# Products of u and v of two chunks written to four row quarters of PSUM instead of two

## Chip, cores and metric

The kernel runs on one core of a Trainium2 chip. The metric is the device time of one execution in microseconds (us); each version is run several times, and the median is compared.

## What is computed

The reference runs a recurrent attention and then two expert networks over its output. Inputs are r, k, v, w, a, b of shape (4, 8, 768, 40): 4 batches, 8 heads, 768 steps, 40 features, all fp32.

```python
for t in range(S):
    y[:, :, t] = np.einsum('bhd,bhde->bhe', rt, state)
    Sa = np.einsum('bhde,bhe->bhd', state, at)
    state = state * wt[:, :, None, :] - np.einsum('bhd,bhe->bhde', Sa, bt)
    state = state + np.einsum('bhd,bhe->bhde', vt, kt)
x = y.transpose(0, 2, 1, 3).reshape(B * S, H * D)
h = max(x @ w1, x @ w2, x @ w3);  x = h @ w_out          # 320 -> 768 -> 320
h = x @ w_in;  x = (h * tanh(softplus(h))) @ w_out       # 320 -> 2048 -> 320
```

## The kernel before

The recurrence is computed in chunks of 32 steps. The 32 pairs of batch and head are handled as two groups of 16, so there are 2 x 24 = 48 chunks, one after the other (`run`, with `chain(c)` for chunk c); the state goes from each chunk to the next. Inside a chunk everything is matmuls on TensorE (PE), with short steps on VectorE (DVE) and ScalarE (ACT) between them. `chain` has five steps, separated by `yield`:

1. x0ps (line 379): the state times the scaled a of each step, 16 matmuls that write to the four row quarters of a PSUM tile in turn; ACT copies the result to X0 (line 382).
2. ups (line 393): X0 times the inverse of a triangular matrix gives u; DVE copies it to ud (line 395).
3. utps (line 404): u transposed; ACT copies it to uT (line 407, two copies) and into the operand rs (line 410, four copies).
4. `products(c, c + 1)` (line 346): for each of the 16 heads the product of r of chunk c with u of chunk c, and the product of r of chunk c + 1 with v of chunk c + 1. Each is a matmul of 40 rows to 32 columns, with 32 columns moving, fp32. All go to the one PSUM tile cgps (one bank of 128 rows x 512 columns). Then DVE multiplies the 64 rows of chunk c by the causal mask and writes them into rs (line 415, "the mask").
5. ys (line 427): 16 matmuls of the keys and the state with rs; their results are the chunk's output (YT, line 434) and the next state (sv, line 432).

The rows of cgps before: chunk c has the 64 rows from 64 x (c mod 2), the products of v in the first 32 of them and of u in the other 32; a head has 32 of the 512 columns. So one call writes to two of the four row quarters, the u of chunk c to one and the v of chunk c + 1 to one in the other half.

Between these steps other work is put by hand, in a fixed order, in the places where the chain would wait ("slots", five per chunk): the preparation of later chunks (`pre`: lines 239 to 283, with m on PE at line 271), the solve of the triangular systems on DVE (`solve`: lines 303 and 305, eight chunks' worth at a time), `kb` (transposed keys, line 320, copied by ACT at line 324), the copies of the state (line 374), the conversion of the expert weights (lines 564 to 596, craw and raw are their loads), and the first expert network (`Moe1`): groups of eight matmuls into a ring of two PSUM buffers bps (lines 645 to 649), read by ACT (line 752) and DVE (line 754), and later the matmuls of line 795. PE, DVE and ACT keep the order of the code; the order on GpSimd (POOL) and on the DMA queue of SyncE (SP) is set by a scheduler. After the last chunk (some 722 us) the rest of the first network and the second one follow.

Of the kernel before, what the change touches and what calls it, by code (L numbers as in the profile page):

```python
# [12 lines left out]
ALU = mybir.AluOpType  # L13
# [4 lines left out]
C = 32  # L18
# [135 lines left out]
class Attention:  # L154
# [184 lines left out]

    def products(self, h, g):  # L340

        for ho in range(16):
            for c, x, row in ((h, self.uT, 32), (g, self.v, 0)):
                if c is not None:
                    row += 64 * (c % 2)
                    self.nc.tensor.matmul(out=self.cg[row:row + 32, C * ho:C * ho + C], lhsT=x[0:40, ho],  # L346
                                          rhs=self.rs[c % 2][0:40, 0:4, ho], start=True, stop=True)

    ZZ = [(jj, zo, 1 - zo // 2, zo % 2) for jj in range(4) for zo in (0, 2, 1, 3)]

    def chain(self, c):
        nc, tc = self.nc, self.tc
# [3 lines left out]
        x, P = self.ax[n % self.NX], self.pp[n % self.NP][0:R].rearrange("r (p c) t -> r p c t", c=2)[:, :, cc]  # L356
        tt = self.tr[self.batch[n] % 2].rearrange("p t i -> p i t")
        i = c % 2
        l, r_, s, u = self.ls[c % 3], self.rs[i], self.sv[i], self.ud
# [17 lines left out]
        for jj, zo, y, g in self.ZZ:  # L377
            K = 104 if y else (128 if g else 96)
            nc.tensor.matmul(out=ps[32 * zo:32 * zo + 32, 40 * jj:40 * jj + 40], lhsT=x[0:K, y, 4 * g + jj, cc],  # L379
                             rhs=s[0:K, y, 4 * g + jj, 0:40], start=True, stop=True)  # L380
# [10 lines left out]
        for jj, zo, y, g in self.ZZ:  # L391
            zr = slice(32 * zo, 32 * zo + 32)
            nc.tensor.matmul(out=ps[zr, 40 * jj:40 * jj + 40], lhsT=tt[zr, item + jj],
                             rhs=X0[zr, 40 * jj:40 * jj + 40], start=True, stop=True)
# [13 lines left out]
        for zo in range(4):  # L408
# [3 lines left out]
        yield  # L412

        self.products(c, c + 1 if c + 1 < 2 * NCH else None)
        nc.vector.tensor_tensor(  # L415
            out=r_[64:128, 0:4], in0=self.cg[64 * i:64 * i + 64].rearrange("p (h b i) -> p b h i", b=4, i=8),
            in1=self.mask[64:128].rearrange("p (b i) -> p b i", b=4).unsqueeze(2).to_broadcast([64, 4, 16, 8]),
            op=ALU.mult)
        yield
        yield  # L420

# [3 lines left out]
        for p in range(8):  # L425
            for y in (1, 0):
                nc.tensor.matmul(out=self.ys[64 * y:64 * y + 40, p, 0:72], lhsT=l[:, y, p],  # L427
                                 rhs=r_[:, :, 4 * (p % 4) + 2 * (1 - y) + p // 4], start=True, stop=True)
        if not last:
            for y in range(2):  # L430
                ro = slice(64 * y, 64 * y + 40)
                nc.vector.tensor_tensor(out=sn[ro, y, :, 0:40], in0=self.ys[ro, :, 32:72],  # L432
                                        in1=P[ro, :, 32:33].to_broadcast([40, 8, 40]), op=ALU.mult)
# [72 lines left out]
    def run(self, fill):  # L506
# [5 lines left out]
        for c in range(NC):  # L512
            n, cc = divmod(c, 2)
            chain = self.chain(c)
            for slot in range(5):
                if slot == 0 and cc == 0 and self.place[n] == 0 and k == self.batch[n]:
                    finish(solve)
                    left = 0
                next(chain, None)
                if slot == 3 and c + 2 < NC:  # L520
                    self.load_v(c + 2)
# [12 lines left out]
                if left > 0:  # L534
                    steps = -(-left // max(1, 5 * (due - c) - slot - 1))
                    for _ in range(steps):
                        next(solve, None)
                    left -= steps
                next(chain, None)
                if cc == 1 and slot in (0, 2) and n + 1 < NT:  # L540
                    self.kb(n + 1, slot // 2)
# [711 lines left out]
```

## Time and profile before

| | |
|---|---|
| median of 3 runs | 1133.1 us (1131.27 to 1139.1) |
| the profiled execution | 1137.88 us, its span 1136.2 us |
| mean granted clock of TensorE | 0.977 of full speed |
| busy over the span | PE 84%, DVE 78%, ACT 64%, POOL 32% |

Durations come from the one profiled execution. PE's matmuls overlap: a record lasts from its start until its result is there, so the pace of a stream is read from start to start, not from durations. A granted clock of 1.00 is 2.4 GHz, 0.50 is 1.2 GHz.

### The profile page before, as it was taken

What the parts mean: (1) busy time and instruction counts of PE and PEld (TensorE: products, weight loads), DVE (VectorE), ACT (ScalarE), POOL (GpSimd) and SP (SyncE); (2) the same over time, 40 slices, a digit from 0 to 9 for tenths busy, and PEclk for the clock granted to TensorE, in tenths of its full rate; (3) what the DMA queues carried; (4) which work ended last, traced back from release to release, by engine and by line L of the source; (5) the groups of instructions that cost most, each with busy time, mean ns of one, the idle gap of its engine ahead of it and who ended that gap; (6) DMA issues with size and microseconds to landing.
All of it is one profiled execution on the core that took longest, in us unless ns stands there. A gap on an engine that the chain in (4) does not pass through costs nothing.

```text
span 1136.2 us, 33971 instructions
## 1 busy us (share of the span) xinstructions
PE 957.3 (84%) x14098; PEld 859.8 (76%) x14098; DVE 882.6 (78%) x1606; ACT 730.8 (64%) x1886; POOL 366.9 (32%) x394
## 2 busy tenths in 40 slices
PE   1334435898999899988999999988999999999996
PEld 1223324787888888888988888888889998989896
DVE  8778689877768785877576665797898989898885
ACT  3447774454455455545546777666878787878885
POOL 7347785233333334333202334474020102010000
PEclk9999999998999899989998999999999999999999
DMA  8234532333334243423323344441010101010000
GB/s 232 89 87 120 149 77 74 71 97 83 87 90 107 64 106 74 117 66 105 88 66 93 98 128 112 135 142 43 1 52 1 52 1 51 1 52 1 24 1 27
DMA packets 110614, 87.02 MB, mean 77 GB/s; under 512 B 72740, under 2 KB 89764, under 8 KB 110452
## 3 DMA queue, kind: packets, MB, share of 16 engines
q1 hardware_dynamic: 109712, 84.54, 27.3%
q8 instruction: 113, 1.85, 0.7%
q14 instruction: 49, 0.40, 0.1%
q10 hardware_dynamic: 740, 0.23, 0.1%
HBM read 72.16 MB, written 12.58 MB: 75 GB/s over the span
## 4 chain that ended last, share of the span: by engine, by line
PE 57%; DVE 21%; ACT 11%; DMA 4%; issue 4%; POOL 2%; SPq 1%; ACTq 0%; DVEq 0%; POOLq 0%
PE cops L971 5%; PE cops L972 5%; PE cops L973 5%; DVE T L305 4%; PE bps L645 4%; PE cps L645 4%; PE cps L646 4%; PE cps L647 4%; PE cgps L346 3%; PE ys L427 3%; PE bps L795 3%; PE bps L646 3%; PE bps L647 3%; DVE tv L303 3%; ACT ls L324 2%
## 5 line engine op out<-in xcount | busy, mean ns | idle before, releaser
L645 PE MATMUL bps<-bxh,bw 128*128 128x256 f32 x432 | 142.7, 331 | 16.5 <-ACT mx L752 8.6
L646 PE MATMUL bps<-bxl,bw 128*128 128x256 f32 x432 | 126.4, 292 | 4.7 <-DVE bxl L658 4.7
L647 PE MATMUL bps<-bxh,bw 128*128 128x256 f32 x432 | 125.1, 290 | 0.0
L305 DVE TENSOR_TENSOR T<-T,tv 128x31 f32<-128x31 f32 (+15 forms) x186 | 104.4, 561 | 6.4
L645 PEld LDWEIGHTS bps<-bxh,bw 128*128 128x128 f32 x432 | 84.4, 195 | 32.1 <-ACT mx L752 16.6
L757 POOL TENSOR_TENSOR hl<-mx,hh 128x256 fp32r<-128x256 f32 x72 | 57.4, 798 | 156.4 <-ACT hh L756 146.9
L427 PE MATMUL ys<-rs,ls 128*40 128x72 f32 x1536 | 67.2, 249 | 33.2 <-ACT t L572 10.7
L646 PEld LDWEIGHTS bps<-bxl,bw 128*128 128x128 f32 x432 | 85.6, 198 | 7.3 <-DVE bxl L658 7.2
L427 PEld LDWEIGHTS ys<-rs,ls 128*40 128x40 f32 x1536 | 58.7, 131 | 39.8 <-ACT t L572 11.0
L647 PEld LDWEIGHTS bps<-bxh,bw 128*128 128x128 f32 x432 | 85.2, 197 | 0.0
L795 PE MATMUL bps<-hh,bo 128*128 128x256 f32 x360 | 77.4, 297 | 6.8 <-DVE mx L754 5.6
L283 POOL TENSOR_SCALAR_AFFINE_SELECT ax<-akT 32x256 f32<-32x256 f32 x96 | 49.2, 513 | 104.8 <-DVE akT L278 100.8
L382 ACT COPY X<-x0ps 128x160 f32<-128x160 f32 x48 | 14.0, 292 | 104.7 <-PE x0ps L379 98.9
L955 ACT ACTIVATE e<-e 128x512 f32<-128x512 f32 x93 | 58.5, 629 | 35.2 <-DVE e L953 34.7
L959 DVE SCALAR_TENSOR_TENSOR e<-e,r 128x512 f32<-128x512 f32 x93 | 75.1, 808 | 7.6 <-ACT r L957 7.6
L303 DVE TENSOR_TENSOR tv<-tr,T 128x31 f32<-128x31 f32 (+15 forms) x186 | 78.3, 421 | 2.3
L754 DVE TENSOR_TENSOR mx<-bps,mx 128x256 f32<-128x256 f32 x144 | 60.4, 420 | 23.3 <-PE bps L649 13.2
L249 POOL TENSOR_TENSOR ax<-ax,pp 40x512 f32<-40x512 f32 x48 | 62.3, 1298 | 49.0 <-DVE tv L303 15.9
L415 DVE TENSOR_TENSOR rs<-cgps,cst 64x512 f32<-64x512 f32 x48 | 33.1, 689 | 58.0 <-PE cgps L346 57.5
L967 DVE TENSOR_TENSOR gl<-e,gh 128x512 fp32r<-128x512 f32 x93 | 64.6, 695 | 16.3 <-ACT gh L966 15.6
L432 DVE TENSOR_TENSOR sv<-ys,pp 40x320 f32<-40x320 f32 x92 | 44.7, 486 | 38.6 <-PE ys L427 37.9
L924 POOL CAST cxh<-cxl 128x1536 fp32r<-128x1536 f32 x5 | 8.3, 1668 | 197.7 <-DMA cxl<-x 197.7
(210 smaller groups left out, 3296.4 us busy)
## 6 DMA issues: line engine op xcount, KB each, us to landing
bk<-in_KB_dram SPq DMA_DIRECT2D x24, 448.0 KB
sv<-in_SV_dram SPq DMA_DIRECT2D x96, 80.0 KB
raw<-in_w_dram SPq DMA_DIRECT2D x18, 384.0 KB
w<-in_W_dram SPq DMA_DIRECT2D x21, 231.0 KB
v<-in_VT_dram SPq DMA_DIRECT2D x48, 96.0 KB
rs<-in_RT_dram SPq DMA_DIRECT2D x48, 96.0 KB
cxl<-x SPq DMA_DIRECT2D x12, 384.0 KB
raw<-in_wo_dram SPq DMA_DIRECT2D x13, 320.0 KB
```

What stands on the lines that cost most here:

```text
L249: nc.gpsimd.tensor_tensor(out=xv, in0=xv, in1=P[ro, :, 0:C], op=ALU.mult)
L303: nc.vector.tensor_tensor(out=tv, in0=abT[:, s, s + 1:C].unsqueeze(2).to_broadcast([128, n, s + 1]), in1=T[:, s, 0:s + 1].unsqueeze(1).to_ ...
L305: nc.vector.tensor_tensor(out=T[:, s + 1:C, 0:s + 1], in0=T[:, s + 1:C, 0:s + 1], in1=tv, op=ALU.subtract)
L427: nc.tensor.matmul(out=self.ys[64 * y:64 * y + 40, p, 0:72], lhsT=l[:, y, p], rhs=r_[:, :, 4 * (p % 4) + 2 * (1 - y) + p // 4], start=True ...
L645: nc.tensor.matmul(out=ps, lhsT=h[:, k], rhs=xh[:, k], start=(k == 0), stop=False)
L646: nc.tensor.matmul(out=ps, lhsT=h[:, k], rhs=xl[:, k], start=False, stop=False)
L647: nc.tensor.matmul(out=ps, lhsT=l[:, k], rhs=xh[:, k], start=False, stop=False)
L754: after(1, lambda ps=ps, mx=mx: nc.vector.tensor_tensor(out=mx, in0=ps, in1=mx, op=ALU.max))
L795: nc.tensor.matmul(out=pss[d][rows], lhsT=lhsT, rhs=rhs, start=first, stop=last)
L955: nc.scalar.activation(out=e, in_=e, func=AF.Square, bias=1.0)
L959: nc.vector.scalar_tensor_tensor(out=e, in0=e, scalar=1.0, in1=r, op0=ALU.add, op1=ALU.mult)
L967: nc.vector.tensor_tensor(out=gl, in0=e, in1=gh.bitcast(F32), op=ALU.subtract)
```

## The change

Heads 0 to 7 and heads 8 to 15 now have their own rows. A product of the first half goes to rows 0 to 63, one of the second half to rows 64 to 127 (v in the first 32, u in the other 32 of each half); chunk c has the 256 columns from 256 x (c mod 2). The loop takes one head of each half in turn, so that four matmuls in a row write to the four row quarters. The mask becomes two instructions, one for each half of the heads.

```diff
--- before.py
+++ after.py
@@ -339,12 +339,14 @@
 
     def products(self, h, g):
 
-        for ho in range(16):
-            for c, x, row in ((h, self.uT, 32), (g, self.v, 0)):
-                if c is not None:
-                    row += 64 * (c % 2)
-                    self.nc.tensor.matmul(out=self.cg[row:row + 32, C * ho:C * ho + C], lhsT=x[0:40, ho],
-                                          rhs=self.rs[c % 2][0:40, 0:4, ho], start=True, stop=True)
+        for k in range(8):
+            for hi in range(2):
+                for c, x, row in ((h, self.uT, 32), (g, self.v, 0)):
+                    if c is not None:
+                        row += 64 * hi
+                        col = 256 * (c % 2) + C * k
+                        self.nc.tensor.matmul(out=self.cg[row:row + 32, col:col + C], lhsT=x[0:40, 8 * hi + k],
+                                              rhs=self.rs[c % 2][0:40, 0:4, 8 * hi + k], start=True, stop=True)
 
     ZZ = [(jj, zo, 1 - zo // 2, zo % 2) for jj in range(4) for zo in (0, 2, 1, 3)]
 
@@ -412,10 +414,12 @@
         yield
 
         self.products(c, c + 1 if c + 1 < 2 * NCH else None)
-        nc.vector.tensor_tensor(
-            out=r_[64:128, 0:4], in0=self.cg[64 * i:64 * i + 64].rearrange("p (h b i) -> p b h i", b=4, i=8),
-            in1=self.mask[64:128].rearrange("p (b i) -> p b i", b=4).unsqueeze(2).to_broadcast([64, 4, 16, 8]),
-            op=ALU.mult)
+        for hi in range(2):
+            nc.vector.tensor_tensor(
+                out=r_[64:128, 0:4, 8 * hi:8 * hi + 8],
+                in0=self.cg[64 * hi:64 * hi + 64, 256 * i:256 * i + 256].rearrange("p (h b i) -> p b h i", b=4, i=8),
+                in1=self.mask[64:128].rearrange("p (b i) -> p b i", b=4).unsqueeze(2).to_broadcast([64, 4, 8, 8]),
+                op=ALU.mult)
         yield
         yield
 
```

The order on PE of the ys matmuls, the last step of the chunk at 557 us (ys is PSUM, rs_157 the masked operand, ls_153 keys and state; behind "waits" stand the engines or DMA queues waited for). Before:

```order
L649 MATMUL bps<-bxl,bw_96 128x256
L427 MATMUL ys<-rs_157,ls_153 40x72 [waits DMAHW7_49,DVE_49,Activation_49]
L427 MATMUL ys<-rs_157,ls_153 40x72 [waits Activation_49]
L427 MATMUL ys<-rs_157,ls_153 40x72 x7
L427 MATMUL ys<-rs_157,ls_153 40x72 [waits Activation_49]
L427 MATMUL ys<-rs_157,ls_153 40x72 x6
L645 MATMUL bps<-bxh,bw_97 128x256 [waits DVE_49]
```

And after the change:

```order
L653 MATMUL bps<-bxl,bw_96 128x256
L431 MATMUL ys<-rs_157,ls_153 40x72 [waits DMAHW7_49,DVE_49,Activation_49]
L431 MATMUL ys<-rs_157,ls_153 40x72 [waits Activation_49]
L431 MATMUL ys<-rs_157,ls_153 40x72 x2
L431 MATMUL ys<-rs_157,ls_153 40x72 [waits DVE_49]
L431 MATMUL ys<-rs_157,ls_153 40x72 x4
L431 MATMUL ys<-rs_157,ls_153 40x72 [waits Activation_49]
L431 MATMUL ys<-rs_157,ls_153 40x72 x6
L649 MATMUL bps<-bxh,bw_97 128x256 [waits DVE_49]
```

The number of ys matmuls is the same. The first waits for DVE as before, and after four of them (1 + 1 + 2) a second wait for DVE has come in: these four read heads 0, 2, 4 and 6, the fifth reads head 8, of the second half.

On DVE, around the mask of the same chunk (cgps holds the products, cst the mask, tv and T_151 belong to the solve). Before:

```order
L303 TENSOR_TENSOR tv<-tr_164,T_151 128x60 [waits DVE_49]
L305 TENSOR_TENSOR T_151<-T_151,tv 128x30x2 [waits DVE_49]
L415 TENSOR_TENSOR rs_157<-cgps,cst 64x512 [waits PE_49]
L754 TENSOR_TENSOR mx<-bps,mx 128x256
L303 TENSOR_TENSOR tv<-tr_164,T_151 128x87 [waits DVE_49]
L305 TENSOR_TENSOR T_151<-T_151,tv 128x29x3 [waits DVE_49]
L432 TENSOR_TENSOR sv_160<-ys,pp_149 40x8x40 [waits PE_49]
```

And after:

```order
L303 TENSOR_TENSOR tv<-tr_164,T_151 128x60 [waits DVE_49]
L305 TENSOR_TENSOR T_151<-T_151,tv 128x30x2 [waits DVE_49]
L418 TENSOR_TENSOR rs_157<-cgps,cst 64x4x64 [waits PE_49]
L418 TENSOR_TENSOR rs_157<-cgps,cst 64x4x64
L758 TENSOR_TENSOR mx<-bps,mx 128x256
L303 TENSOR_TENSOR tv<-tr_164,T_151 128x87 [waits DVE_49]
L305 TENSOR_TENSOR T_151<-T_151,tv 128x29x3 [waits DVE_49]
L436 TENSOR_TENSOR sv_160<-ys,pp_149 40x8x40 [waits PE_49]
```

One mask instruction has become two in the same place; the first waits for PE, for the last product that either of them needs, and the second waits for nothing more.

On SP, where a late weight load is issued (craw is its target, xs the stored attention output, bxl its reload for the first network, sv the next chunk's input). Before:

```order
L336 DMA rs_157<-in_VI_dram 32x640 [waits DMAHW2_49]
L564 DMA craw<-in_wi_dram 128x768 [waits DMAHW3_49,Activation_49,Pool_49]
L442 DMA xs_4_68<-YT 320x1x64 [waits DMAHW4_49,DVE_49]
L442 DMA xs_4_68<-YT 320x1x64 [waits DMAHW5_49]
L716 DMA bxl<-xs_3_67 128x2x256 [waits DMAHW6_49,PE_49]
L718 DMA bxl<-xs_3_67 64x256 [waits DMAHW7_49]
L718 DMA bxl<-xs_3_67 64x256 [waits DMAHW0_49]
L338 DMA sv_160<-in_SV_dram 64x8x40 [waits DMAHW1_49,PE_49]
```

And after:

```order
L336 DMA rs_157<-in_VI_dram 32x640 [waits DMAHW2_49]
L446 DMA xs_4_68<-YT 320x1x64 [waits DMAHW3_49,DVE_49]
L446 DMA xs_4_68<-YT 320x1x64 [waits DMAHW4_49]
L720 DMA bxl<-xs_3_67 128x2x256 [waits DMAHW5_49,PE_49]
L722 DMA bxl<-xs_3_67 64x256 [waits DMAHW6_49]
L722 DMA bxl<-xs_3_67 64x256 [waits DMAHW7_49]
L568 DMA craw<-in_wi_dram 128x768 [waits DMAHW0_49,Activation_49,Pool_49]
L338 DMA sv_160<-in_SV_dram 64x8x40 [waits DMAHW1_49,PE_49]
```

The weight load has moved behind the two stores of xs and the three loads of bxl. In three places near the beginning a weight load (raw) has moved behind one or two neighbours in the same manner, and one store (x) behind one load.

## Rows read from the trace of the kernel before

**Rows 1.** The page, engines: busy us (share of the span) x instructions.

```profile
PE 957.3 (84%) x14098; PEld 859.8 (76%) x14098; DVE 882.6 (78%) x1606; ACT 730.8 (64%) x1886; POOL 366.9 (32%) x394
```

**Rows 2.** Table by stretches: length, busy us of each engine (x), clock, DMA.

```profile
200.00:722.00 522.00, 488.95 (x10013) 440.70 (x10015) 370.19 (x773) 299.49 (x951) 170.31 (x199) 0.96 0.35 92
```

**Rows 3.** Chain that ended last: shares in 200 to 722; pieces (start, length).

```profile
by line: PE bps L645 8.7%; PE cgps L346 7.6%; PE ys L427 7.2%; PE bps L795 6.9%; DVE T L305 6.1%; PE bps L646 5.9%; PE bps L647 5.4%; ACT ls L324 3.9%; issue 3.7%; PE m L271 3.5%; ACT ls L374 3.0%; PE bps L648 2.7%; PE bps L649 2.7%; DVE sv
...
92.06 4.58 DMA raw<-in_w_dram
...
282.28 1.70 PE cgps L346 x60
...
323.30 0.71 DVE rs L415
...
557.28 1.13 PE cgps L346 x64
...
614.71 1.85 PE cgps L346 x64
```

**Rows 4.** Line 346, whole span: durations min/median/max in ns; who waited (us, times).

```profile
L346 PE MATMUL cgps<-rs,uT x1536: 192/193/260, 67.2 to 720.4; 40*32 40x32 f32 x192
...
  DVE rs L415: 57.5, 33
```

**Rows 5.** Timeline of PE at 557 us: start us, length us.

```profile
557.21 0.21 PE L346 MATMUL cgps<-rs,uT 40*32 40x32 f32 x1
557.22 0.21 PE L346 MATMUL cgps<-rs,v 40*32 40x32 f32 x1
...
558.22 0.19 PE L346 MATMUL cgps<-rs,v 40*32 40x32 f32 x1
558.35 0.38 PE L645 MATMUL bps<-bxh,bw 128*128 128x256 f32 x1
...
559.28 0.28 PE L649 MATMUL bps<-bxl,bw 128*128 128x256 f32 x1
559.49 1.20 PE L427 MATMUL ys<-rs,ls 128*40 128x72 f32 x32
```

**Rows 6.** Timeline of PE, last chunk, records merged.

```profile
719.44 1.19 PE L346 MATMUL cgps<-rs,uT 40*32 40x32 f32 x32
720.57 0.39 PE L645 MATMUL bps<-bxh,bw 128*128 128x256 f32 x1
```

**Rows 7.** Timeline of PE at 501 us, first step of a chunk, records merged.

```profile
501.76 0.49 PE L379 MATMUL x0ps<-sv,ax 104*32 104x40 f32 x32
502.18 0.40 PE L368 MATMUL ys<-cst,sv 40*104 40x40 f32 x8
```

**Rows 8.** Groups of DVE by shape, 200 to 722: busy us, mean ns, idle before.

```profile
L754 DVE TENSOR_TENSOR mx<-bps,mx 128x256 f32<-128x256 f32 x122 | 51.3, 420 | 16.0 <-PE bps L649 8.0 <-ACT mx L752 6.9
...
L415 DVE TENSOR_TENSOR rs<-cgps,cst 64x512 f32<-64x512 f32 x42 | 29.0, 689 | 57.8 <-PE cgps L346 57.5
```

**Rows 9.** Timeline of DVE at 558 us (in brackets idle before, releaser).

```profile
558.46 0.70 DVE L415 TENSOR_TENSOR rs<-cgps,cst 64x512 f32<-64x512 f32 x1 [1.97 <-PE cgps L346]
```

**Rows 10.** Table by stretches, columns as in rows 2 (clock third from the end).

```profile
279.20:288.30 9.10, 9.10 (x168) 8.42 (x170) 3.01 (x7) 3.00 (x9) 0.85 (x1) 0.50 0.13 38
...
310.00:330.00 20.00, 18.46 (x399) 16.42 (x392) 14.07 (x30) 11.42 (x35) 6.97 (x10) 1.00 0.36 98
```

**Rows 11.** Timeline of PE: two waits in the solve stretches.

```profile
277.12 0.39 PE L645 MATMUL bps<-bxh,bw 128*128 128x256 f32 x1 [1.85 <-DVE mx L754]
...
327.84 0.39 PE L645 MATMUL bps<-bxh,bw 128*128 128x256 f32 x1 [1.16 <-ACT mx L752]
```

**Rows 12.** Timeline of SP and of ACT at 658 to 666 us.

```profile
658.68 0.35 SPq L564 DMA_DIRECT2D craw<-in_wi_dram  x1
...
661.44 1.81 SPq L718 DMA_DIRECT2D bxl<-xs  x2
...
665.66 0.55 ACT L571 ACTIVATE ct<-craw 128x384 f32<-128x384 f32 x1
```

## The prediction

> **What bounds the kernel now.** I first read the engine totals of the page [rows 1]: TensorE (PE) is busy 84% of the span, VectorE (DVE) 78%. That is an average over stages, so I cut the span next. The table by stretches [rows 2] shows that from 200 to 722 us, where the attention chunks run beside the first expert network, PE is busy 489 of 522 us and DVE only 370: there PE is the tight engine, though not everywhere. Then the chain that ended last [rows 3]: in this stretch the products of line 346 hold 7.6% of it, 0.076 x 522 = 39.7 us. Followed piece by piece in short windows, the chain passes through the products of 33 chunks: 28 pieces of about 1.0 to 1.16 us (the piece at 557.28 is one), three of about 1.70 us (at 282.28, and alike in the chunks at 386 and 492), one of 1.53 us (chunk 6), one of 1.85 us (at 614.71). In nine chunks after the sixth it goes round them, through DVE's solve (lines 303 and 305) or ScalarE (ACT). The first six chunks hang on DMA, GpSimd and DVE; their products are not on the chain, only their masks are.
>
> The same is seen from DVE: its mask (line 415) waits for the products 33 times, 57.5 us together [rows 4], so 1.7 us each time.
>
> **The products.** A call issues 32 fp32 matmuls, and the trace records two passes for each: 1536 records of u over 48 calls [rows 4], as many of v, so 64 records a call. In the call of the chunk at 557 us [rows 5] u and v start in pairs, and the 64 records go from 557.21 to 558.22: 1.01 us, or 32 ns between two records of one row quarter (32 of each), 16 ns between any two. What sets that pace? The last chunk says it [rows 6]: it has no v part, 32 records all in one quarter, and it takes as long, 1.19 us with the last record's 0.19 (the length of one record [rows 5]), so 1.00 us for the starts. Half the records in half the quarters at one pace: each quarter is a lane of its own. And the first product of each chunk (x0ps, line 379) already writes to all four quarters in turn, with records that are longer (40 columns against 32): 32 records in 0.49 us, less a last record of about 0.20, is 0.29/31 = 9 ns between starts [rows 7]. After the change u and v of one head in each half write to four different quarters, 16 records in each: 16 x 32 ns = 0.51 us for the 64. A call loses 0.50 us of 1.01. The 0.13 us between the last start and the next line's first matmul [rows 5] stays.
>
> On the chain: 28 x 0.50 = 14.0 us; the three pieces of 1.70 us lie where the granted clock is 0.50, the lower level of 1.2 GHz [rows 10], and halve to 0.85: 2.6 us; chunk 6: 0.77 us; the piece of 1.85 us, less its 0.17 us of fixed end at that clock, halves: 0.84 us. Sum 18.2 us. Bounds: from nothing, if the pace of 16 ns were that of instructions, to 0.50 us more in each of the nine chunks that the chain goes round, 4.5 us; I take the middle case, which the rows of lines 346 and 379 show directly.
>
> **The mask.** One DVE instruction of 64 x 512 becomes two of 64 x 256. The row of 512 elements takes 689 ns, a two-input row of 256 elements that also reads PSUM takes 420 ns [rows 8]. So two cost 840 ns, 0.15 us more, 0.16 with a start between them. The exact form is not in the trace; from below two halves can cost 689 ns together (nothing more), from above 689 each (0.69 us more). I take 0.16, since line 754 is the nearest row. Cover: where DVE waited for the products (1.7 us a time [rows 4]), DVE itself can afford it. What it delays is line 427 (ys) on PE. In the chunk at 557 us the mask starts at 558.46 and lasts 0.70 us [rows 9], so it ends at 559.16; PE reaches ys at 559.49 after the eight matmuls of the ring [rows 5]: 0.33 us of cover. Two halves end 0.16 us later, and only the fifth matmul of ys needs the second half, so no wait there. Where the cover fails is where the mask stands on the chain itself: fifteen pieces (the first six chunks and nine later; the one at 323.30 is such [rows 3]): 15 x 0.16 = 2.4 us. With 0.69 it would be 10.4 us.
>
> **What moves beside it.** The order on ACT and GpSimd is the same, PE and DVE keep theirs but for the changed lines. On SP a weight load moves behind neighbours in three places of the first 130 us, by about the length of one or two issues; there the w load stands behind ACT, not behind SP, and I cost it at nothing. Late in the attention a weight load (craw) goes behind five issues: it was issued at 658.68 and would follow the loads that end at 663.25; ACT reads it at 665.66 [rows 12]. The only comparable landing in a chain, 384 KB at 92.06 [rows 3], took 4.58 us: 663.3 + 4.6 = 667.9, so ACT could stand 2.3 us. Bounds 0 to 2.3; that landing belongs to a stretch of dense DMA, so I take 0 and keep 2.3 in the range.
>
> **The sum.** -18.2 + 2.4 = -15.8 us. The profiled execution took 1137.9 us and would take 1122.1. It lies 4.8 us above the median of three runs, 1133.1; applied there: 1117.3, say 1117 us. Own range of this case: the best end has 18.2 + 4.5 = 22.7, masks at nothing: 1110; the worst end has masks at 10.4 and SP at 2.3, 18.2 - 12.7 = 5.5: 1128.
>
> A measurement of this kernel can tell about 1%, 11.3 us, from no change: below 1121.8 is faster.
>
> **Rivals.**
> *Another chain close behind takes half.* For it: in the solve stretches DVE is late anyway. Most of the nine chunks that the chain leaves out are there, and PE already waits there (1.85 us before line 645 at 277.12, 1.16 us at 327.84 [rows 11]); a PE that comes earlier only waits longer. Against it: after such a wait the chain returns to PE, and the long run from 550 to 722 us has PE on it almost throughout. If half of 15.8 is given back: 1125 us. Chance 0.20.
>
> *The pace is that of instructions, not of quarters.* Then 64 records keep 16 ns and only the masks are left: 1133.1 + 2.4 = 1135.5 us. For it: no row shows this very tile shape in four quarters; 40 rows against the 104 of line 379. Against it: rows 6 and 7. Chance 0.05. The Trainium skill, TensorEngine Tiling (Array Packing), section on performance considerations, has the rule that would make it so: every matmul carries about 60 cycles of overhead however few columns it has, so a dimension that is already small should not be tiled. By that rule a call could not fall below 64 x 25 ns = 1.6 us, an estimate from that page at 2.4 GHz. This trace disagrees already: 1.01 us for 64 records [rows 5], 9 ns a record in line 379 [rows 7].
>
> *The clock falls more often: slower.* PE's wait of 1.85 us [rows 11] is followed by a stretch at a granted clock of 0.50, 279.20 to 288.30; the wait of 1.16 us is not, the clock stays at 1.00 from 310 to 330 [rows 10]. The change takes 0.5 us of PE work from before each such wait and lengthens the DVE side by 0.16, so waits of 1.2 to 1.3 us grow towards 1.8. There are five of this kind between 300 and 540 us (the one at 327.84 is one). A stretch of 10 us at half clock costs 5 us of PE time, so it decides from four new stretches on: 4 x 5 = 20 against 15.8; with five 1133.1 - 15.8 + 25 = 1142 us. Against it: the chain reaches most of these waits through the same products, so that both sides move and the wait hardly grows. Chance 0.05.
>
> **How the numbers follow.** Forecast 0.67; half given back 0.20; instruction pace 0.05; clock 0.05; better than forecast, because the chunks off the chain gain too or a half-clock stretch vanishes, 0.03. Faster by over 1%: 0.67 x 0.93 + 0.20 x 0.35 + 0.03 = 0.72. Slower by over 1%: most of the clock's 0.05, 0.04. The rest, 0.24, within 1%. For 8 in 10 the range takes the forecast's own and most of the half case: 1109 to 1129 us.
>
> **What would show it.** Right: a full call's 64 starts in about 0.5 us, records about 8 ns apart; the masks at about 420 ns each, 0.85 us together; the share of the products in the chain falls from 7.6% to about 4%; ys not waiting for the second mask in the chunks after 550 us; attention ending about 16 us earlier, and the rest of the program as long as before. Wrong: starts still 16 ns apart (instruction pace); masks near 0.69 us each; waits on PE before lines 645 and 795 grown by what the products lost (another chain); more stretches at a granted clock of 0.50 between 300 and 600 us (clock).

## The result, and the profile after

The change makes the kernel faster by 1.07%: 1123.31 us median of 4 runs (1116.3 to 1123.94) against 1133.89 us of the kernel before (1131.27 to 1139.1), ratio 0.9893, 95% interval [0.9861, 0.9925], so 12.1 us [8.5, 15.8]. Measured twice more, beside other kernels, it gave 0.9864 [0.9837, 0.9892] and 0.9898 [0.9872, 0.9925]. The forecast was 1117 us, a ratio of 0.986: the sign and the mechanism hold, the gain is 0.4 to 4.2 us smaller by the three ratios. The profiled execution took 1123.92 us, its span is 1122.2 us.

The page's engine row and the table by stretches of the kernel after, with the columns of [rows 1] and [rows 2]:

```profile
PE 934.1 (83%) x14098; PEld 834.6 (74%) x14098; DVE 889.4 (79%) x1654; ACT 731.2 (65%) x1886; POOL 367.0 (33%) x394
...
200.00:722.00 522.00, 484.00 (x10123) 432.56 (x10124) 387.55 (x836) 309.23 (x979) 179.42 (x209) 0.96 0.37 96
```

PE has the same 14098 instructions and is busy 23.2 us less (957.3 to 934.1); DVE has 48 more and is busy 6.8 us more. Of PE's 23.2 us only half or so reached the end of the program.

The timeline of PE, kernel after, in the chunk that stood at 557 us before (chunk 33, counted from 0; compare [rows 5]), and the last chunk ([rows 6]):

```profile
547.68 0.21 PE L348 MATMUL cgps<-rs,uT 40*32 40x32 f32 x1
547.69 0.21 PE L348 MATMUL cgps<-rs,v 40*32 40x32 f32 x1
547.70 0.21 PE L348 MATMUL cgps<-rs,uT 40*32 40x32 f32 x1
547.70 0.21 PE L348 MATMUL cgps<-rs,v 40*32 40x32 f32 x1
...
548.25 0.19 PE L348 MATMUL cgps<-rs,v 40*32 40x32 f32 x1
548.37 0.38 PE L649 MATMUL bps<-bxh,bw 128*128 128x256 f32 x1
...
549.51 1.20 PE L431 MATMUL ys<-rs,ls 128*40 128x72 f32 x32
...
704.89 0.69 PE L348 MATMUL cgps<-rs,uT 40*32 40x32 f32 x32
```

The 64 starts take 0.57 us (0.56 in most chunks in which no other matmul stands between them) where they took 1.01: 8.9 ns from one to the next. The last chunk, 32 records in two quarters, takes 0.69 - 0.19 = 0.50 us where it took 1.00 in one. From the last start to ys it is 1.26 us, before 1.27: in this chunk ys does not wait for the second mask.

The mask in the kernel after: DVE's timeline in the same chunk (in brackets idle before and its releaser), and the view of its line (durations min/median/max in ns; then who was waited for, us and times):

```profile
548.48 0.88 DVE L418 TENSOR_TENSOR rs<-cgps,cst 64x256 f32<-64x256 f32 x2 [1.52 <-PE cgps L348]
```

```profile
L418 DVE TENSOR_TENSOR rs<-cgps,cst x96: 417/423/430, 73.2 to 706.1; 64x256 f32<-64x256 f32 x96
...
  PE cgps L348: 41.5, 30
```

Two masks take 0.88 us together, 0.19 more than the one of 0.69 [rows 8]. DVE waits for the products 41.5 us instead of 57.5 [rows 4], though its masks are longer.

The chain of the kernel after, 200 to 714 us (to the end of the attention): shares by line, then pieces (start, length):

```profile
by line: PE bps L649 9.1%; PE bps L799 7.3%; PE ys L431 7.3%; DVE T L305 6.4%; PE bps L650 5.9%; PE bps L651 5.5%; issue 5.1%; PE cgps L348 4.7%; PE m L271 3.4%; ACT ls L324 3.0%; DVE mx L758 2.9%; PE bps L652 2.8%; PE bps L653 2.8%; ACT ls
...
280.56 0.85 PE cgps L348 x47
...
320.52 0.42 DVE rs L418
320.97 0.44 DVE rs L418
...
547.75 0.69 PE cgps L348 x50
...
602.89 1.01 PE cgps L348 x64
```

The products fell from 7.6% [rows 3] to 4.7%: 0.047 x 514 = 24.2 us against 39.7. The piece at half clock went from 1.70 to 0.85 us, the one of 1.85 us to 1.01. That is 15.5 us off the chain; some 3 us of it came back as masks and as waits. The waits of PE in 200 to 722 us show the latter (line waited for: us in total, times, longest), first the kernel before, then after:

```profile
PE bps L645 <- ACT mx L752: 8.6, 10, 1.8
PE bps L795 <- DVE mx L754: 5.6, 6, 1.3
PE bps L645 <- DVE mx L754: 5.6, 3, 1.9
```

```profile
PE bps L649 <- ACT mx L756: 9.5, 9, 2.0
PE bps L799 <- DVE mx L758: 7.2, 6, 1.5
...
PE bps L649 <- DVE mx L758: 6.8, 7, 1.9
```

The three together grew from 19.8 to 23.5 us.

### The profile page after: what moved, and what is told of

It is laid out like the page before. It is cut to its first block, busy times and chain, and to the rows that moved or that the text cites. A ratio compares the mean times of both kernels' runs of the same rounds, so it can differ in the third digit from the quotient of the medians.

```text
span 1122.2 us, 34018 instructions
## 1 busy us (share of the span) xinstructions
PE 934.1 (83%) x14098; PEld 834.6 (74%) x14098; DVE 889.4 (79%) x1654; ACT 731.2 (65%) x1886; POOL 367.0 (33%) x394
## 3 DMA queue, kind: packets, MB, share of 16 engines
q8 instruction: 113, 1.85, 0.7%
## 4 chain that ended last, share of the span: by engine, by line
PE 57%; DVE 17%; ACT 6%; issue 3%; DMA 1%; DVEq 0%; ACTq 0%; POOL 0%; SPq 0%
PE cops L977 5%; PE cops L975 5%; PE cops L976 5%; PE bps L649 5%; DVE T L305 4%; PE cps L650 4%; PE cps L649 4%; PE cps L651 4%; PE bps L799 3%; PE ys L431 3%; PE bps L650 3%; PE bps L651 3%; PE cgps L348 2%; PE cps L652 2%; PE cps L653 2%
## 5 line engine op out<-in xcount | busy, mean ns | idle before, releaser
L418 DVE TENSOR_TENSOR rs<-cgps,cst 64x256 f32<-64x256 f32 x96 | 40.6, 423 | 43.6 <-PE cgps L348 41.5
L436 DVE TENSOR_TENSOR sv<-ys,pp 40x320 f32<-40x320 f32 x92 | 44.7, 486 | 31.4 <-PE ys L431 30.7
```

## Where in the attention the time was won

Whole spans hide this: two executions of the change differ by 3.0 us in the first 175 us, and by some us in stretches at half clock. So the experiments are read in stretches from the first x0ps of one chunk to that of a later one. Such a stretch is seen in the view of x0ps (first and last start behind the durations), here from the first record of chunk 32 to the first few of chunk 38, in the kernel before, after, and in the experiment e10:

```profile
L379 PE MATMUL x0ps<-sv,ax x200: 202/202/223, 540.0 to 607.0; 104*32 104x40 f32 x100
```

```profile
L381 PE MATMUL x0ps<-sv,ax x200: 202/202/223, 530.9 to 595.4; 104*32 104x40 f32 x100
```

```profile
L381 PE MATMUL x0ps<-sv,ax x205: 202/202/223, 528.7 to 595.3; 104*32 104x40 f32 x103
```

Six chunks take 67.0, 64.5 and 66.6 us. The table gives such stretches for all kernels, in us, worked out from the first record of each chunk; in brackets the us at a granted clock of 0.50, where there are any. Chunks 14 to 20 run beside the solve on DVE, 32 to 38 without it.

```
                      chunks 8-12   14-20         22-28         32-38         40-46
before                47.76         74.43         75.68 (3.4)   66.97         67.61
the change            47.03         72.88         74.42 (3.4)   64.45         65.61
  again (e1)          47.08         74.32 (3.4)   73.13         64.43         66.35 (3.4)
  third time (e11)    47.10         72.86         73.16         64.42         65.61
e2 masks alone        47.79         75.82 (3.4)   77.37 (6.8)   67.05         67.57
e3 one mask           46.76         72.39         72.67         64.39         65.53
e4 half the products  46.58         74.88 (6.8)   72.64         62.75         64.60
e5 ys by halves       48.57 (3.4)   76.68 (10.2)  75.29 (3.4)   64.42         66.46
e6 products twice     50.16         79.85 (3.4)   77.84         70.13 (1.7)   73.86 (3.4)
e7 half the solve     44.97         69.95         71.19 (3.4)   65.77 (3.4)   65.68
e8 both halves        44.35         70.52 (3.4)   69.27         62.71         64.57
e9 mask ahead         47.56 (2.5)   72.38         73.11         64.99         65.61
e10 two quarters      47.46         73.92         76.88 (6.8)   66.46         67.32
```

Without a bracket, three executions of the change agree within 0.07 us. A chunk gained (66.97 - 64.43) / 6 = 0.42 us in 32 to 38, (74.43 - 72.87) / 6 = 0.26 in 14 to 20, 0.33 in 40 to 46 and 0.17 in 8 to 12. A call became 0.45 us shorter. Chunk by chunk, each against those executions of the change that have the same time at half clock in it, chunks 5 to 46 give 11.5 us: 5.6 us in 8 to 31, 5.5 us in 32 to 46.

## Experiments

**The change once more, and its two parts.** Three kernels on one chip, beside the kernel before (1132.49 us). The first is the change as it is.

> The changed kernel as it is, timed in five rounds beside the kernel before. Forecast: 15.8 us less than the kernel before, ratio 0.986. The first timing gave 0.989 (10.6 us less), with an interval that holds both. Theory A (the sum is right to within 2 us, the rest is the spread between executions): ratio 0.985 to 0.988. Theory B (a third of the gain is taken by another chain that lies close behind): ratio 0.989 to 0.991.

1118.9 us, ratio 0.9864 [0.9837, 0.9892]: in the range of theory A. The first and the third measurement, 0.9893 and 0.9898, lie in that of B and the intervals overlap, so the ratios do not decide; the 11.5 us from single chunks are nearer to B, two thirds of 15.8.

The second is the kernel before with its mask in two halves:

```diff
-        nc.vector.tensor_tensor(
-            out=r_[64:128, 0:4], in0=self.cg[64 * i:64 * i + 64].rearrange("p (h b i) -> p b h i", b=4, i=8),
...
+        for hi in range(2):
+            nc.vector.tensor_tensor(
+                out=r_[64:128, 0:4, 8 * hi:8 * hi + 8],
+                in0=self.cg[64 * i:64 * i + 64, 256 * hi:256 * hi + 256].rearrange("p (h b i) -> p b h i", b=4, i=8),
...
```

> The kernel before with only the mask split in two (heads 0 to 7, heads 8 to 15; the products stay in two quarters). The trace of the changed kernel shows 0.88 us for two masks against 0.69 for one, 0.19 more. Theory A: the price falls only where the mask is on the chain, fifteen times in the kernel before, 15 x 0.19 = 2.9 us: ratio 1.0025. Rival (it falls in each of the 48 chunks): 9 us, ratio 1.008. Rival (the first mask lets ys start earlier): 1 to 3 us less than before, ratio 0.998.

1130.27 us, 0.9983 [0.9962, 1.0005]: nothing that can be told from no change, in the stretches too (+0.03, +0.08, -0.04 where no bracket stands). But its two masks are not those of the change. DVE's timeline of e2 in chunk 13:

```profile
292.17 0.77 DVE L416 TENSOR_TENSOR rs<-cgps,cst 64x256 f32<-64x256 f32 x2
```

Both read the same 64 rows here, the second starts 0.08 us before the first has ended, and the two take 0.75 to 0.77 us, 0.06 to 0.08 more than one. In the change they read different rows, 0.03 us lie between them, and the two take 0.88. So e2 shows that masks in two parts are not the gain of the change, but it does not test the price of 0.19 us; why the two forms differ, no run tells.

The third is the change with one mask of 64 x 512 in every chunk but the first:

```diff
-        for hi in range(2):
+        if c:
+            nc.vector.tensor_tensor(
+                out=r_[64:128, 0:4], in0=self.cg[0:64].rearrange("p (h b i) -> p b h i", b=4, i=8),
...
+        for hi in range(0 if c else 2):
```

> The changed kernel with one mask instruction of 64 x 512 from the second chunk on, which reads the products of heads 0 to 7 of both chunks in place of those of heads 0 to 15 of one (so the products of heads 8 to 15 are left out of the output). The four quarters without the price of the split. Theory A: 33 pieces of the chain lose 0.45 us and five of them twice that, about 17 us less than the kernel before, ratio 0.985, some 3 us under the changed kernel. Rival (another chain close behind): about the time of the changed kernel, within 1 us, since what the mask gives back is not on the chain.

1115.98 us, 0.984 [0.9815, 0.9864], 2.9 us under the change, as theory A has it, but with intervals that overlap. The groups of DVE by shape, 200 to 722 us, e2 and then e3 (busy us, mean ns of one, idle before):

```profile
L416 DVE TENSOR_TENSOR rs<-cgps,cst 64x256 f32<-64x256 f32 x84 | 31.9, 418 | 58.0 <-PE cgps L346 57.7
```

```profile
L418 DVE TENSOR_TENSOR rs<-cgps,cst 64x512 f32<-64x512 f32 x42 | 28.7, 684 | 41.7 <-PE cgps L348 41.2
```

The stretches say where it would lie: 14 to 20 is 0.48 us shorter than with two masks, 22 to 28 0.48, 8 to 12 0.31, and 32 to 38 only 0.04. So the second mask costs mainly beside the solve, where DVE is late, and later in single chunks (0.60 us in chunk 39). Chunk by chunk at equal clock it is 1.7 us in chunks 5 to 46. The gain of the change comes from the products.

**Are quarters the lanes?** The same instructions and masks, with the two halves of the heads one after the other:

```diff
-        for k in range(8):
-            for hi in range(2):
+        for hi in range(2):
+            for k in range(8):
```

> Same instructions and same masks as the change, but the two halves of the heads one after the other: first all products of heads 0 to 7 (u and v in two row quarters), then all of heads 8 to 15 (the other two). If each row quarter is a lane of its own at 32 ns a record, two quarters at a time give 16 ns between starts again: the 64 records of a call start in about 1.0 us, and the time is that of the kernel before (1130 to 1135 us; the first mask may start half a call earlier, which could win up to 3 us of it back). Rival, the gain of the change comes from the masks in halves or from the new places in PSUM and not from four quarters in turn: starts stay at 0.56 us, time as the change, about 1119 us.

1127.7 us, 0.9962 [0.9939, 0.9985]. The timeline of PE, e10, chunk 33:

```profile
545.75 0.21 PE L348 MATMUL cgps<-rs,uT 40*32 40x32 f32 x1
545.76 0.21 PE L348 MATMUL cgps<-rs,v 40*32 40x32 f32 x1
545.80 0.19 PE L348 MATMUL cgps<-rs,uT 40*32 40x32 f32 x1
545.81 0.19 PE L348 MATMUL cgps<-rs,v 40*32 40x32 f32 x1
545.84 0.19 PE L348 MATMUL cgps<-rs,uT 40*32 40x32 f32 x1
...
546.15 0.19 PE L348 MATMUL cgps<-rs,uT 40*32 40x32 f32 x1
546.16 0.19 PE L348 MATMUL cgps<-rs,v 40*32 40x32 f32 x1
546.16 0.21 PE L348 MATMUL cgps<-rs,uT 40*32 40x32 f32 x1
546.17 0.21 PE L348 MATMUL cgps<-rs,v 40*32 40x32 f32 x1
...
546.67 0.19 PE L348 MATMUL cgps<-rs,v 40*32 40x32 f32 x1
```

u and v start in pairs every 0.03 us again, and a call takes 0.92 us. The pair of 0.21 us at 546.16 is the first of the other two quarters (the first record of a quarter is longer, as at 545.75): by then 13 of the 16 records of u of the first quarter have started, so three rounds run beside the next two quarters: 3 x 0.031 = 0.09 us, by which the call is under 1.01. The order alone, with all else kept, gives back most of the gain: chunks 32 to 38 lose 2.03 of the 2.54 us. So four quarters in turn are the change, and neither the masks nor the new places. The time lies 2 us under the expected 1130 to 1135, within the 3 us allowed for, but the reason named there does not hold: the first mask starts 0.24 us behind the last product, as before the change. 42 calls x 0.09 = 3.8 us would be enough.

**What a shorter or longer call is worth.** From the third call on only heads 0 to 3 and 8 to 11:

```diff
-        for k in range(8):
+        for k in range(4 if h is not None and h > 1 else 8):
```

> The changed kernel whose products, from the third call on, are issued for half the heads only (0 to 3 and 8 to 11; the products of the other heads are left out, old values stand in their place). A call falls from 0.56 to about 0.28 us of starts. Theory A (the products are on the chain in some 31 chunks): 31 x 0.28 = 8.7 us less than the changed kernel. Rival (another chain lies close behind): 4 us less or nothing.

1113.98 us, 0.9832 [0.9807, 0.9856], 4.9 us under the change: on the rival's side. A call's 32 starts take 0.26 us. Chunks 32 to 38 get 1.68 us, 0.28 each, nearly all of the 0.30 that the call loses; 40 to 46 get 0.17 each, 8 to 12 0.12, 22 to 28 0.08. Beside the solve most of what PE saves is lost again; what holds these chunks, e7 shows below.

And every product twice:

```diff
-        for k in range(8):
+        for k in [*range(8)] * 2:
```

> The changed kernel that issues each product twice, the second time over the first (the output stays the same). A call takes 0.56 us more of PE. Theory A (products on the chain in some 31 chunks): 17 us more than the changed kernel. Rival (in the solve stretches DVE is the bound, so PE has room there): full price, 0.56 us a chunk, only from the thirty-first chunk on and before the eleventh, nothing or half in between: 11 to 13 us more. The trace tells where.

1157.25 us, 1.0221 [1.019, 1.0251]: some 38 us over the change, twice the theory and three times the rival. A call's 128 starts take 1.10 us, 0.54 more. The rest stands in the waits of PE, e6, 200 to 722 us:

```profile
PE ys L431 <- issue: 7.6, 12, 1.8
PE m L271 <- issue: 6.1, 8, 1.0
```

In the change these are 2.5 us for ys and none for m ("issue" is time in which PE waits for nothing that the profile shows). From chunk 5 to chunk 47 e6 takes 556.4 us and the change in e1 522.9, both with 37.5 us at half clock: 33.5 us. 42 x 0.54 = 22.7 for the records and 7.6 - 2.5 + 6.1 = 11.2 for these waits make 33.9, which is close in part by luck, since the price is not the same everywhere. Chunks 33, 34, 37, 45 and 46 take 0.52 to 0.56 us more than in e1, the full price of the call. Chunks 11, 13, 19, 21, 27 and 29 take nothing more (within 0.02 us): there PE has room, as the rival says. Others take more than the price; in some of them stand the issue waits, which neither theory has. Why the additional instructions bring them, no run tells.

**What stands close behind.** Every second step of the solve left out (both its instructions), in the change and in e4:

```diff
+            if s % 2 == 0:
...
-            nc.vector.tensor_tensor(out=T[:, s + 1:C, 0:s + 1], in0=T[:, s + 1:C, 0:s + 1], in1=tv, op=ALU.subtract)
+                nc.vector.tensor_tensor(out=T[:, s + 1:C, 0:s + 1], in0=T[:, s + 1:C, 0:s + 1], in1=tv, op=ALU.subtract)
```

> The changed kernel with every second step of the solve on DVE left out (lines 303 and 305 for odd s; the triangular inverse is incomplete). DVE loses about 15 us of work per eight chunks in the solve stretches. Theory A (there DVE is a chain close behind PE, which took what the products gave): chunks 11 to 30 get faster by 1 to 3 us per eight chunks beyond the changed kernel, some 5 to 10 us in all, and fewer stretches at the lower clock; chunks 31 to 47 keep their pace. Rival (PE alone is the bound): no difference but for the clock.

> The kernel with half the solve steps (as in e7) and half the products (as in e4), both left out. Against e7 a call loses 0.28 us. In the run with half the products and the whole solve, chunks 13 to 28 gained nothing over the changed kernel. Theory A (DVE held them): with half the solve these chunks gain too, 0.2 to 0.28 us each, so 9 to 12 us less than e7 in place of 5. Rival (something other than DVE's solve holds them, ACT or the matmuls' own waits): again nothing between chunks 13 and 28.

1070.51 us, 0.9454 [0.9435, 0.9473], and 1063.47 us, 0.9383 [0.9362, 0.9403]. With half of DVE's steps gone, chunks 14 to 20 take 2.9 us less than in the change, 0.5 us a chunk, and 40 to 46 as long as there: DVE sets the pace beside the solve and not after it. It is plainest in the six chunks that e6 left as they were: 11, 19 and 27 take 12.9 us and 13, 21 and 29 take 11.9 us (12.0 once) in the change, with half the products and with twice as many, and 11.5 and 11.0 us with half the solve. In all e7 gained over 45 us where its theory had 5 to 10: its execution reaches chunk 5 at 158.9 us in place of 173.4 to 176.4, and has 6.8 us at half clock from chunk 5 to 47 in place of 23.9 to 37.5. Halving the products then brings 0.16 us a chunk in 8 to 12 (0.12 with the whole solve) and 7.0 us in all, less than the 9 to 12 expected but more than the 4.9 with the whole solve. In the stretches between chunks 14 and 38 one of the two always has a bracket, so how much more the calls bring there stays open.

**Two attempts at more.** ys takes the first half of the heads first, so that it waits later for the second mask:

```diff
-        for p in range(8):
+        for p in (0, 1, 4, 5, 2, 3, 6, 7):
```

> The changed kernel with the ys matmuls in another order: first those of heads 0 to 7, then those of heads 8 to 15, so that the second mask is needed by the ninth matmul in place of the fifth. Theory A (the split mask costs through ys, which waits for the second half): up to 0.26 us in each of the eleven chunks where the mask is on the chain, 1 to 3 us less than the changed kernel. Rival (behind the mask the chain goes on inside DVE, to lines 754 and 253): no difference, within 1 us.

1121.57 us, 0.990 [0.9863, 0.9936]: no gain. Yet ys does wait for the second mask beside the solve. In all three executions of the change its fifth matmul starts 0.19 us behind the last record of the fourth in chunks 9, 11, 13, 17, 19, 21, 25, 27 and 29, in the others from chunk 7 on, at full clock, 0.03 to 0.06; in e5 the 0.19 us are gone in all nine. PE's timeline of ys in chunk 17, the change and then e5:

```profile
345.04 1.36 PE L431 MATMUL ys<-rs,ls 128*40 128x72 f32 x32
```

```profile
344.12 1.20 PE L431 MATMUL ys<-rs,ls 128*40 128x72 f32 x32
```

The 0.16 us are not kept: chunks 17 and 18 together take 23.18 us in e5 and 23.21 in the change, and 11, 13, 19, 27 and 29 are as long as there within 0.03 us. So the rival holds: behind the mask the chain goes on inside DVE.

No solve steps in the third slot of a chunk, so that the masks come ahead of them on DVE; and beside it the change a third time:

```diff
                     steps = -(-left // max(1, 5 * (due - c) - slot - 1))
+                    if slot == 2:
+                        steps = 0
```

> The change with no solve steps in the third slot of a chunk, so that on DVE the masks stand ahead of them and the steps follow in other slots. Theory, in chunks 9, 13, 17, 21, 25 and 29 the 0.45 us that the products save is given back because the masks come behind a solve step and are 0.2 us longer in two parts: with the masks ahead these chunks keep it, 6 x 0.45 = 2 to 3 us less than the change, about 1116 us. Rival, what those chunks wait for is DVE's total work between two states and not its order: the moved steps make the state (sv) late by as much, time as the change within 1 us, or longer.

> The change once more, beside the two others on the same chip: 1117 to 1121 us, ratio 0.986 to 0.990. It gives the spread between two calls and is the base that the other two are compared with; no theory hangs on it.

e9 took 1126.22 us, 0.9941 [0.9918, 0.9963], the change 1121.44 us, 0.9898 [0.9872, 0.9925]. In place the theory is right: chunks 9 to 11, 17 to 19 and 25 to 27 are 0.47 to 0.54 us shorter than in the change, 13 and 29 0.27 to 0.29. But 22 to 28 stay as they were in all, 32 to 38 are 0.55 us longer, and the moved steps pile up ahead of chunk 8. PE's timeline there, e9, then the table by stretches:

```profile
222.16 0.39 PE L651 MATMUL bps<-bxh,bw 128*128 128x256 f32 x1 [2.59 <-ACT mx L758]
```

```profile
219.80:223.20 3.40, 1.04 (x7) 1.04 (x8) 3.04 (x6) 1.52 (x3) 1.11 (x2) 0.93 0.10 29
223.20:226.60 3.40, 3.40 (x51) 2.88 (x50) 0.42 (x1) 1.82 (x7) 2.95 (x2) 0.56 0.35 73
```

PE stands 2.59 us while DVE is busy 3.04 of 3.40 us, and right after it the clock is at 0.56. From chunk 7 to chunk 8 e9 falls 2.6 us behind the change of its batch. So those chunks gain as the theory says, and the moved steps cost more elsewhere, as the rival says. How much of the 4.8 us is the clock is not separated: from chunk 5 to 47 the profiled executions have 44.4 and 23.9 us at half clock. No version with the whole work was found that beats the change.

## Why the prediction was right, and where its size was off

**Quarters as lanes: right.** The step from [rows 6] and [rows 7] to "each quarter is a lane of its own" holds in the change, in its last chunk and in e10. The term was mis-sized: "16 x 32 ns = 0.51 us for the 64" measured 0.56, on average 35 ns a round of a quarter. A call lost 0.45 us, not 0.50: 33 x 0.05 = 1.7 us of the sum.

**Which chunks gain: nearly right.** At full clock a call is 0.44 to 0.49 us shorter in every chunk (before against e11), and then some chunks give it back. The nine that the chain went round (9, 11, 13, 19, 21, 25, 27, 29, 41) kept nothing or almost nothing: 9 and 25 lost it at ys and at the next wait before line 645, 19 is shorter by 0.23 us because of another wait. The step that failed is that the other 33 keep all: 17, 39 and 42 lost it too, at ys or at the waits before lines 645 and 795. 3 x 0.45 = 1.4 us.

**The mask: right in part of its places, a little small.** Two masks take 0.19 us more, not 0.16; fifteen pieces would make 2.9 us, forecast 2.4. Against e3, chunk by chunk, the nine pieces named after the sixth chunk (7, 9, 13, 15, 21, 25, 29, 31, 39) are not alike: 9, 13, 21, 25 and 29 cost 0.18 to 0.25 us each (over the chunk and the next), 39 0.60, and 7, 15 and 31 next to nothing. Not named were 17 (0.20), 37 (0.18) and 11, 19 and 27 (some 0.1 each). Of the first six only chunk 5 can be read, 0.18. The cover named for the chunks after 550 us held for ys in all of them; beside the solve ys waits for the second mask in nine chunks (e5).

**SP: right.** ACT's first reading of the weight load that moved late in the attention did not wait for it, and no new DMA wait is among those of PE. The three moves near the beginning cannot be read, since three executions of the change reach chunk 5 at 173.4, 173.5 and 176.4 us. After the attention the program is as long as before: from the first x0ps of the last chunk to the end 422.0 us before, 422.6 us after.

Put together: 18.2 - 1.7 - 1.4 - 2.9 = 12.2 us, against 12.1, 15.4 and 11.6 us by the three ratios and 11.5 us by single chunks. That it comes so near is in part luck, as some pieces of the mask cost nothing and others were not named.

**The profiled execution and the median: a weak step.** The sum was made against an execution 4.8 us over the median and carried over whole. Some 3.5 us of that lie ahead of chunk 5, which came at 177.0 us in it and at 173.1 to 174.8 us in those of e1 to e6 and e9 to e11, where executions of one kernel differ by as much as 3.0 us.

**The rivals.** *Another chain close behind takes half* was half a truth: it takes the whole gain in single chunks, most of them beside the solve, and leaves nearly all of it in 32 to 38; of the forecast 15.8 us about a fifth went in all, 1.4 us of it this way. *The pace of instructions* fell: 8.9 ns a record. By the Trainium skill's rule of about 60 cycles for each matmul (TensorEngine Tiling (Array Packing), Performance Considerations) no call could have become shorter than 1.6 us, an estimate by that page; the trace disagrees: it is nearly three times too long. *The clock falls more often*: not shown. From chunk 5 to 1000 us the kernel before has 47.8 us at a granted clock of 0.50, the change 47.8, 47.8 and 30.7 us in its three profiled executions. Its price, 5 us for 10 us at half clock, is the upper end of what is seen: 3.4 us cost the change 1.45 us in chunks 14 to 20, 1.28 in 22 to 28 and 0.74 in 40 to 46 (rows with a bracket against those without), and chunk 28 takes 17.74 us with 10.2 us at half clock (e1) but 14.18 and 14.71 with 3.4, so 2 to 5 us for 10.

## What to carry to other kernels

When small matmuls write to fewer than four row quarters of PSUM, look at the starts within one quarter, not at those of any two: if they stand at the quarter's own pace, a loop order that takes the four quarters in turn nearly halves the stream, and the order matters as much as the places do. Count the gain chunk by chunk along the chain, and expect it whole only where no other engine is late; where one is, work taken from PE and work added to it can both leave the time as it was, as in six chunks here, so a run with twice the work tells where PE has room. To measure a few tenths of a us, compare the same stretch at the same clock rather than the whole program.

## What was not expected of the hardware

**A round costs a little more with four quarters.** Start to start within a quarter it is 52 to 53 ns at first and then 31 to 32 with one or two quarters at work; with four it is the same in the first half of a call and then 33 to 34, after one step of 42. From 64 to 128 records a call grows from 0.56 to 1.10 us, 8.4 ns a record. The Trainium skill (TensorE: Matmul & The Clock Gate, Wait — 56ns, not 53.3ns?) has no two starts closer than about 25 ns; within a quarter the trace agrees, with 31 ns and more, between quarters it does not, with 8.9 ns.

**The clock differs between executions of the same program.** The table by stretches, 200 to 722 us, of the change in e11 (the row of the first execution stands with the result), and one stretch of the first execution:

```profile
200.00:722.00 522.00, 484.21 (x10104) 433.14 (x10096) 393.26 (x841) 312.78 (x992) 185.18 (x215) 0.98 0.37 98
```

```profile
508.70:512.10 3.40, 3.40 (x53) 3.18 (x54) 1.53 (x5) 2.83 (x10) 0.43 (x1) 0.50 0.65 140
```

0.96 in the one and 0.98 in the other, 37.5 and 23.9 us at half clock from chunk 5 to 47. The stretch at 508.70 follows a PE wait of 1.50 us; in the other two executions PE has the same wait of 1.50 us there, and the clock stays at 1.00. Single executions of one kernel lie 9 us apart in e11 (1115.26 to 1124.5 us) without any difference in their work; how much of that is the clock, the one profiled execution does not tell.
